# Constant scales for all f16 halves with one verdict at the end, a new order for batch 0, and batch 2's attention weights as f16 halves

## The chip, the cores and the metric

One NeuronCore of a Trainium2 chip runs the whole program. The metric is the time of one execution on the device in microseconds, the median of several runs. In the profile PE is TensorE (matmul), PEld its weight loads, DVE VectorE, ACT ScalarE, POOL GpSimd and SP SyncE, whose queue issues nearly all DMAs.

## The reference

```python
# q, k, v: (8, 12, 448, 64) f32; w_in: (768, 2048), w_out: (2048, 768) f64
scores = scale * np.matmul(q, k.transpose(0, 1, 3, 2)) - np.log(S)
attn = 1.0 / (1.0 + np.exp(-scores))
x = np.matmul(attn, v)             # then (8 * 448, 768)
h = x @ w_in
g = h - np.tanh(h)
out = g @ w_out
```

Attention with a sigmoid in place of a softmax feeds a two-layer product. h is small here, so h - tanh(h) needs far more than f16's precision, and the weights come as f64.

## The kernel before

A factor of a product is held either as f32, or as two f16 halves, high = f16(s·t) and low = f16(s·t - high), with a scale s. A product of two factors in halves takes three f16 matmuls (high·high, high·low, low·high), a product of f32 factors one f32 matmul, which the trace shows as two instructions. Making halves takes two elementwise operations: the high part (`split`, `parts`, `prep_v`, `halves`, mostly on ACT, some on DVE) and the low part (a SCALAR_TENSOR_TENSOR on DVE).

The scale of every such tensor is computed from its data. For w_in and w_out, `conv_end` sums absolute values or columns with a matmul for each converted piece (`cs`, L303, 24 pieces; `wl`, L297, 32 pieces), and `w_in_scales`, `w_out_scale` and `scale_of` make a power of two from it. For q, k and v, `norm` takes sums of squares on ACT, and `scales` makes the scales of two head pairs with a matmul (`pbn`, L478) and a chain of small DVE operations. For x, `token_norms` (`nm`, L826) and `x_scale` do it, for g `g_scales`. The scales are tiles of [128, 1], which the operations read as operands.

The program runs batch after batch. In batch 0 (`first`) the weights come in and are turned from f64 to f32 (`convert`: `conv_load`, `conv_sign` on ACT, `conv_bits` on DVE), while batch 0's attention runs in f32 (`attention32`). Then `mixture` makes g from eight blocks of w_in: the first FP32 = 6 blocks with f32 matmuls (L1264), the other two with f16 halves (`product`, L953), for which x and w_in are split before. `moe2` is the second product (`po`, L1156). From batch 1 on, `moe2` of batch b is interleaved with the attention of batch b+1 (`stream`, cut into steps called blocks), and the first product is done by `moe1` (batch 1) or `moe1_quarters` (from batch 2 on, `py`, `px`, L1003), which reads w_in's combinations from DRAM into a ring (`load_ring`, L158). `combine` makes these combinations during batch 1.

AV32 = 3 says that in batches 0, 1 and 2 the attention weights times v are f32 matmuls (the `a`, `vn` form of L559). From batch 3 on the weights are split (`split_a`, L545 and L546) and v too (`prep_v`), and three f16 matmuls take the place of one.

Each engine runs its instructions in program order. What sets that order: for batch 0 the string ORDER, one letter a step (s scores, v weights times v, r a piece of w_in, R a piece of w_out, M half a block of the mixture, t a step of g's curve, q halves of x, S and Z halves of w_in, A and a halves of w_out, P a part of moe2, B a step of the next batch's attention, C a late piece of w_out, n, w, y, g, x, b, X steps of the scales); for the others the tables BLOCKS, BLOCKS1, TAIL, MADE, FILL and PARTS, which give the place of a step among moe2's matmuls in microseconds. Scores and the mixture's blocks share two PSUM buffers (`sc`): a block's buffer comes free when both ACT (`u`, L1119) and DVE (`m`, L1121) have read it.

At the end `verdict` compares the largest h with a limit, and a flag decides whether `General`, a slow f32 version of everything, runs after it.

Of the kernel before, what the change touches and what calls it, by code (L numbers as in the profile page):

```python
# [20 lines left out]
D = 64  # L21
QT = 3
A_SCALE = 2.0**15
TINY = 2.0**-120
CUT = 0.65


# [9 lines left out]
class Builder:  # L37

    AV32 = 3

    EARLY = 4
    LAND = ("o", "o", 2, "v", "v", "v", 1, 0, 3, 4, 5, "o", "o", 2, "v", "v", "v", 1, 0, "o")
    ORDER = (
        "lurmlorumsrrsrrmmlussmvvrrssvvrlrssvvrrvruvlssrurssvvrrssvlrrsvvvursrsvs"
        "vrrssvrsrrvvvvRrRrRRRMrRRRnRrRRGMRRwtMttRtRBtwRRtMwBgttMtRtRttDMBttRtRtt"
        "DMtyqqMBBtRttqRqMtBttqqMttSSDMtRxStRtBRAStMtttSADMtBttSMttAttAttMMtAPPta"
        "RRBPtBbtCaBCBACPtFCCPBPCPPBPPCBCPPBCBCPPCCBPCCCPBCCCPCXBaaAPaPPPBAPaaaBB"
        "PPSPSZPSZSPPPPPPSPBPPZPPPNPZPSPZSSNNPPSZPZSSPPPP"
# [3 lines left out]
    TAIL = (1, 2, 4.5, 5)  # L52
    MADE = (6, 9, 12.5, 15, 18, 22, 25, 29, 31, 34)
# [5 lines left out]
    BLOCKS1 = (4, 7, 8, 11, 13, 16, 20, 20, 20, 27, 32, 36, 36, 36, 43, 47, 51, 52)  # L59

    TP = 8
    FP32 = 6
# [3 lines left out]
    AWAY = (1, 3)  # L66

# [3 lines left out]
    def __init__(self, ctx, tc, q, k, v, w_in, w_out, out):  # L71
# [20 lines left out]
        self.ident = self.const.tile([P, P], F32, name="ident")  # L92
        make_identity(nc, self.ident)
        self.identb = self.const.tile([P, P], BF16, name="identb")
        nc.vector.tensor_copy(self.identb, self.ident)
        self.onesf = self.const.tile([P, P], F32, name="onesf")
        nc.vector.memset(self.onesf, 1.0)
# [80 lines left out]
    def combine(self):  # L178
# [74 lines left out]
    def conv_sign(self, p):  # L253
# [7 lines left out]
        else:  # L261
            pool, tag, bufs = self.xp, "x", 8
            if p["when"] == "mixture" and p["k"] % 3:
                pool, tag, bufs = (self.xp, "x2", 2) if p["k"] % 3 == 1 else (self.nat, "vn", 2)
# [21 lines left out]
    def conv_end(self, p):  # L286


        nc = self.nc
        kind, r, i, n = p["piece"]  # L290
        high = p["a"].bitcast(BF16).rearrange("p (n t) -> p n t", t=2)[:, :, 1]
        if kind == "out":
            start = r == (self.EARLY if p["when"] == "product" else 0)
            stop = r == (self.EARLY - 1 if i and p["when"] == "mixture" else self.NF - 1)
            if start:
                self.wl = self.ps.tile([P, 512], F32, name="wl", tag="mm", bufs=2)
            nc.tensor.matmul(self.wl[:, :n], self.onesb, high, start=start, stop=stop)  # L297
            if stop:
                self.sums_out[i].append(self.wl)
            return  # L300
        if r == 0:
            self.cs = self.ps.tile([P, 512], F32, name="cs", tag=("av", "tr")[i % 2], bufs=1)
        nc.tensor.matmul(self.cs[:, :n], self.identb, high, start=(r == 0), stop=(r == self.NC - 1))  # L303
        if r == self.NC - 1:
            sq = self.sm.tile([P, n], BF16, name="sq", tag="sq", bufs=4)
            nc.scalar.activation(sq, self.cs[:, :n], AF.Square)
            self.row.append(sq)

    def convert(self, pieces, when):

        ps = [{"piece": q, "k": k, "when": when} for k, q in enumerate(pieces)]
        wait, end = [None, None], [None, self.conv_end]
        if when == "mixture":
            wait, end = [None] * 3, [None] + end
        elif when == "product":
            wait, end = [None], [None, None] + end
        stages = [self.conv_load] + wait + [self.conv_sign, self.conv_bits] + end
# [23 lines left out]
    def split_w_in(self):  # L341

        for n in range(0, self.NC * self.NB, 2):
            self.split_rows(self.wi, n, self.Swi)
            yield 1

    def scale_of(self, total, tag, unit=2.0**49):

        nc = self.nc
        t = self.sm.tile([P, 1], F32, name=tag + "_t")  # L350
        nc.vector.tensor_scalar(t, total, 2.1, TINY, op0=ALU.mult, op1=ALU.max)
        y = self.pow2(t, 1, tag)
# [1217 lines left out]
```

## Time and profile before

| | |
|---|---|
| median of 3 runs | 1125.9 us (1125.8 to 1128.17) |
| the profiled execution | 1125.58 us, span 1123.7 us |
| PE busy | 1113.8 us (99%) |
| DVE, ACT, POOL busy | 780.3, 781.9, 70.8 us |
| from the start to the first mixture matmul | 50.7 us |
| mixture, then moe2 of batch 0, to 215.4 us | 164.7 us |
| moe1 of batch 1, to 269.9 us | 54.5 us |
| moe2 of batch 1 with batch 2's attention, to 361.8 us | 91.9 us |

The span goes from the first instruction to the last. Busy time of PE is modelled, since matmuls overlap in the array; the time from one matmul's start to the next says more. A row of the timeline that stands for several instructions gives their first start and their total.

### The profile page before, as it was taken

Reading aid. Unit: us, or ns where it says so; the run is one execution under the profiler, and the core shown is the slowest. Engines: PE = TensorE matmul, PEld = TensorE weight load, DVE = VectorE, ACT = ScalarE, POOL = GpSimd, SP = SyncE. Lnnn points to the kernel's source line nnn. Section 1 sums busy time; section 2 is a strip of 40 time slices with the busy share of each in tenths; the row PEclk is TensorE's granted clock in tenths of the full one; section 3 lists DMA queues with packets and bytes.
Section 4 is the critical chain, followed back from the end, with each engine's and each line's share of the span. In section 5 each row is a group of like instructions: output and inputs, shape, how many; then the busy total and the mean of one; then the engine's idle time right before and its main releaser. Section 6 shows DMA issues by size and latency. Waiting matters only on the chain.

```text
span 1123.7 us, 20080 instructions
## 1 busy us (share of the span) xinstructions
PE 1113.8 (99%) x8067; PEld 671.8 (60%) x8072; DVE 780.3 (69%) x1376; ACT 781.9 (70%) x1269; POOL 70.8 (6%) x54
## 2 busy tenths in 40 slices
PE   9999999999999999999999999999999999999997
PEld 3355444554445984469644894449844696449953
DVE  6989888697466666787578865887768775655710
ACT  7967895466777569886788767886698867655600
POOL 0000000000000002200021000200022000200000
PEclk9999999999999999999999999999999999999999
DMA  9992262284544742236324543247512670036200
GB/s 367 393 361 63 88 196 71 87 230 131 188 161 161 250 164 69 75 111 241 115 67 131 182 148 129 72 162 242 185 59 75 201 256 21 17 99 230 99 25 28
DMA packets 78694, 167.13 MB, mean 149 GB/s; under 512 B 24320, under 2 KB 58240, under 8 KB 71808
## 3 DMA queue, kind: packets, MB, share of 16 engines
q1 hardware_dynamic: 78304, 165.42, 43.7%
q8 instruction: 65, 1.06, 0.4%
q10 hardware_dynamic: 288, 0.34, 0.1%
q14 instruction: 37, 0.30, 0.1%
HBM read 137.43 MB, written 28.31 MB: 147 GB/s over the span
## 4 chain that ended last, share of the span: by engine, by line
PE 89%; DVE 7%; ACT 2%; issue 1%; DMA 1%; DVEq 0%; SPq 0%; ACTq 0%
PE po L1156 35%; PE py L1003 12%; PE px L1003 10%; PE acc L559 9%; PE sc L528 9%; PE ph L953 6%; PE ph L1264 5%; DVE wi L334 3%; DVE ahl L546 2%; DMA wi<-w 1%; ACT sqn L469 1%; PE cs L303 1%; PE warm L115 1%; ACT a L539 1%; PE wl L297 1%
## 5 line engine op out<-in xcount | busy, mean ns | idle before, releaser
L1156 PE MATMUL po<-g,wo 128*128 128x448 f16 x2304 | 451.9, 353 | 0.0
L1156 PEld LDWEIGHTS <-wo 128*128 128x128 f16 x2304 | 219.3, 98 | 221.7 <-issue 26.7
L1003 PEld LDWEIGHTS <-wi 128*128 128x128 f16 x3024 | 289.8, 98 | 6.6 <-issue 1.5
L546 DVE SCALAR_TENSOR_TENSOR ahl<-a,ahl 128x896 f16<-128x896 f32 x105 | 135.0, 1320 | 95.4 <-ACT ahl L545 94.3
L539 ACT ACTIVATE a<-sc,nls,rn 128x896 f32<-128x896 f32 x147 | 155.7, 1089 | 59.0 <-PE sc L528 58.9
L1003 PE MATMUL py<-wi 128*128 128x224 f16 x1728 | 181.8, 259 | 1.9 <-DMA wi<-w 1.0
L1003 PE MATMUL px<-wi 128*128 128x224 f16 x1296 | 140.4, 259 | 0.0
L947 DVE SCALAR_TENSOR_TENSOR g<-m,Sg,g 128x896 f16<-128x896 f32 x64 | 73.6, 1150 | 44.7 <-ACT g L946 44.6
L528 PE MATMUL sc<-Q,K 64*128 64x448 f16 x1008 | 100.6, 353 | 0.0
L545 ACT ACTIVATE ahl<-a 128x896 f16<-128x896 f32 x105 | 94.3, 941 | 0.5
L1013 ACT ACTIVATE u<-py,ih 128x448 f32<-128x448 f32 x48 | 30.4, 634 | 77.7 <-DVE py L1084 77.7
L946 ACT ACTIVATE g<-m,Sg 128x896 f16<-128x896 f32 x64 | 66.2, 1034 | 13.6 <-DVE m L1027 11.1
L528 PEld LDWEIGHTS <-K 64*128 64x128 f16 x1008 | 35.5, 97 | 58.6 <-issue 34.5
L559 PE MATMUL acc<-ahl,vhl 128*64 128x448 f16 (+1 forms) x720 | 67.2, 356 | 0.0
L590 POOL TENSOR_TENSOR x<-x 128x448 f32<-128x448 f32 x20 | 22.8, 1139 | 599.1 <-ACT x L573 599.1
L1264 PE MATMUL ph<-x,wi 128*128 128x448 f32 x144 | 55.8, 540 | 0.0
L1016 DVE SCALAR_TENSOR_TENSOR m<-px,ihk,u 128x448 f32<-128x448 f32 x48 | 32.8, 683 | 32.6 <-ACT u L1013 32.6
L953 PEld LDWEIGHTS <-wi 128*128 128x128 f16 x360 | 35.2, 98 | 33.2 <-issue 0.5
L953 PE MATMUL ph<-xhl,wi 128*128 128x448 f16 x288 | 54.6, 352 | 0.0
L559 PE MATMUL acc<-a,vn 128*64 128x448 f32 (+1 forms) x288 | 54.4, 553 | 0.0
L599 POOL TENSOR_TENSOR x<-x,x 128x448 f32<-128x448 f32 x21 | 35.3, 1682 | 298.3 <-ACT x L588 297.1
L1027 DVE SCALAR_TENSOR_TENSOR m<-q,m 128x896 f32<-128x896 f32 x48 | 52.0, 1084 | 0.7
(186 smaller groups left out, 1218.3 us busy)
## 6 DMA issues: line engine op xcount, KB each, us to landing
wi<-w SPq DMA_DIRECT2D x53, 1344.0 KB, 6.1
out<-o SPq DMA_DIRECT2D x47, 224.0 KB, 2.0
knn<-k SPq DMA_DIRECT2D x45, 224.0 KB, 2.6
qnn<-q SPq DMA_DIRECT2D x44, 224.0 KB, 3.1
rawo<-moe_w_out SPq DMA_DIRECT2D x23, 384.0 KB, 4.7
raw<-moe_w_in SPq DMA_DIRECT2D x13, 512.0 KB, 8.2
vn<-v SPq DMA_DIRECT2D x24, 256.0 KB, 2.9
w<-wi SPq DMA_DIRECT2D x16, 384.0 KB, 5.9
```

The lines of the kernel that those rows point to most:

```text
L528: self.nc.tensor.matmul(ps[i * m : (i + 1) * m, h, : self.S], K[i][r, w, c * P : c * P + m], Q[i][r, x, :], start=(n == 0), stop=(n == len ...
L539: self.nc.scalar.activation(a[:, 0], ps[:, :, : self.S], AF.Sigmoid, bias=self.nls, scale=scale)
L545: nc.scalar.activation(A[:, 0], a[:, 0], AF.Copy, scale=A_SCALE)
L546: nc.vector.scalar_tensor_tensor(A[:, 1], a[:, 0], A_SCALE, A[:, 0], op0=ALU.mult, op1=ALU.subtract)
L559: self.nc.tensor.matmul(acc[i][h * D : (h + 1) * D, : self.S], v[k, w, 2 * QT + h if half else h * QT + c], A[k, x, h], start=(n == 0 and ...
L946: nc.scalar.activation(g[:, 0], m, AF.Copy, scale=Sg)
L947: nc.vector.scalar_tensor_tensor(g[:, 1], m, Sg, g[:, 0], op0=ALU.mult, op1=ALU.subtract)
L953: self.nc.tensor.matmul(ph, self.wi[:, self.slot(c, k), part, e * P : (e + 1) * P], xhl[c][:, x, :], start=(i == 0), stop=(i == len(prods) ...
L1003: nc.tensor.matmul(out, w[:, a, c, i], x[:, b, c, j], start=start and k == 0, stop=k == len(prods) - 1, skip_group_check=True,)
L1027: V.scalar_tensor_tensor(d["m"], d.pop("q"), C0, d["m"], op0=ALU.add, op1=ALU.mult)
L1156: nc.tensor.matmul(po[:, :S], self.wo[:, e * self.NF + rows[f // 2][f % 2], w, at : at + P], moving(gs[f // 2][:, x], f % 2), start=(f == ...
L1264: nc.tensor.matmul(ph[:, e, :S], self.fp32(self.wi, self.slot(c, k))[:, 0, e * P : (e + 1) * P], xs[c], start=(c == 0), stop=(c == self.NC ...
```

## The change

All scales become constants of the class: KQ = 2^6 for q and k, VS = 2^8 for v, XS = 2^12 for x, WS = 2^10 for w_in, OS = 2^11 for w_out and GS = 2^22 for g. With them go `conv_end`, `pow2`, `scale_of`, `w_in_scales`, `w_out_bound`, `w_out_scale`, `scales`, `x_scale`, `h_scales` and `g_scales`. The sums of squares of q, k and v stay, but go to a tile `seen` that only `verdict` reads; those of v are now taken in batch 1 too, and those of w_out by eight squares in the last batch (`check_w_out`). `verdict` has eight conditions instead of one.

The operations that read a scale from a tile now have it as a number in the instruction. The high halves of q and k move: ten of 84 stay on ACT (QA, KA), the others are on DVE (before: all 42 of q and 4 of k on ACT). The squares of x that POOL multiplied and added are now made on ACT and added on DVE in pairs (`squares`). AV32 becomes 2 and FP32 becomes 4, with ORDER and BLOCKS1 rewritten.

```diff
-    AV32 = 3
+    AV32 = 2
+    QA = (1, 2, 4, 6, 8)
+    KA = (0, 1, 4, 5, 11)
...
-    FP32 = 6
+    FP32 = 4
...
+    KQ = 2.0**6
+    VS = 2.0**8
+    XS = 2.0**12
+    GS = 2.0**22
+    WS = 2.0**10
+    OS = 2.0**11
...
-    def conv_end(self, p):
...
-            nc.tensor.matmul(self.wl[:, :n], self.onesb, high, start=start, stop=stop)
...
-        nc.tensor.matmul(self.cs[:, :n], self.identb, high, start=(r == 0), stop=(r == self.NC - 1))
...
-    def scales(self, ss, where):
...
-    def add_squares(self, j, x, pool):
+    def squares(self, j, x, b):
...
+            if j % 2 == 0:
+                self.x2 = self.xp.tile([P, 2, self.S], BF16, name="x2", tag="x2", bufs=3)
+            x2 = self.x2[:, j % 2]
+        self.nc.scalar.activation(x2, x, AF.Square)
...
+        elif j % 2:
+            self.nc.vector.tensor_tensor(self.x2s, self.x2s, self.x2, op=ALU.add)
...
-                K[g] = self.parts(qk[g][0], sc[g][0][:, 0:1], "K", g < NP and g not in (2, 3))
+                K[g] = self.parts(qk[g][0], self.KQ, "K", g in self.KA)
...
-                Q[g] = self.parts(qk[g][1], sc[g][0][:, 1:2], "Q", True)
+                Q[g] = self.parts(qk[g][1], self.KQ, "Q", g in self.QA)
...
-            aa = [self.weigh(pss[0], sc[g][1][:, 0:1])]
+            aa = [self.weigh(pss[0], weight)]
...
+    def check_w_out(self):
...
+            self.nc.scalar.activation(
+                t, self.wo[:, i * n : (i + 1) * n, 0], AF.Square, accum_out=self.seen_out[:, i : i + 1]
+            )
...
-            events.append((20, self.verdict))
+            checks = self.check_w_out()
+            events += [(6 + 4 * n, lambda: next(checks)) for n in range(self.NF // 2)]
+            events.append((42, self.verdict))
```

PE in a stretch of batch 0's attention (sc scores, acc weights times v, cs the matmul of `conv_end`), before:

```order
L559 MATMUL acc<-a_242,vn 64x448 x2
L559 MATMUL acc<-a_247,vn 64x448 x2
L303 LDWEIGHTS identb
L303 MATMUL cs<-sta,identb 128x512
L303 LDWEIGHTS identb
L303 MATMUL cs<-sta,identb 128x512
L559 MATMUL acc<-a_282,vn 64x448 x2
```

and now:

```order
L480 MATMUL acc<-a_224,vn 64x448 x2
L480 MATMUL acc<-a_229,vn 64x448 x2
L480 MATMUL acc<-a_262,vn 64x448 x2
L480 MATMUL acc<-a_267,vn 64x448 x2
L449 MATMUL sc<-qnn,knn 128x448 x4
L449 MATMUL sc<-qnn,knn 64x448 x2
```

The cs matmuls that stood between the matmuls of attention are gone.

DVE in the mixture (m and g are the curve's steps and its low half, stb and wo the conversion of w_out, wi the low half of w_in, un to rn the scales of q and k), before:

```order
L933 TENSOR_SCALAR g_765<-g_765 128x1
L122 TENSOR_SCALAR g_y<-g_765 128x1
L936 TENSOR_SCALAR iSg<-g_y 128x1
L938 RECIPROCAL Sg<-iSg 128x1
L1121 SCALAR_TENSOR_TENSOR m<-ph,ihk_117,u 128x896
L947 SCALAR_TENSOR_TENSOR g<-m,Sg,g 128x896
L1127 SCALAR_TENSOR_TENSOR m<-q,m 128x896
```

and now:

```order
L986 SCALAR_TENSOR_TENSOR m<-ph,u 128x896
L815 SCALAR_TENSOR_TENSOR g<-m,g 128x896
L992 SCALAR_TENSOR_TENSOR m<-q,m 128x896
L305 SCALAR_TENSOR_TENSOR wi<-wi 128x2x256
L268 SCALAR_TENSOR_TENSOR stb<-stb,rawo 128x384
L276 SCALAR_TENSOR_TENSOR wo<-rawo,stb 128x384
L305 SCALAR_TENSOR_TENSOR wi<-wi 128x2x256 x2
```

The one-column operations are gone, and more halves of w_in stand between the curve's steps: from the first m<-ph to the eighth there are 98 instructions before and 72 now; 13 instead of 6 of them are halves of w_in.

ACT in batch 2's attention (a the sigmoid, ahl the high half of a weight tile, sqn the sums of squares), before:

```order
L571 ACTIVATE x_2954<-acc 128x448
L588 ACTIVATE x_2956<-x_2954 128x448
L539 ACTIVATE a_2978<-sc,nls,rn 128x896
L503 ACTIVATE Q<-qnn,sn 128x448
L469 ACTIVATE sqn,ss_121<-knn 128x448
```

and now:

```order
L494 ACTIVATE x_2820<-acc 128x448
L508 ACTIVATE x_2822<-x_2820 128x448
L466 ACTIVATE ahl<-a_2781 128x896
L466 ACTIVATE ahl<-a_2786 128x896
L1038 ACTIVATE o<-po 128x448
L460 ACTIVATE a_2867<-sc,nls 128x896
L424 ACTIVATE K<-knn 128x448
L466 ACTIVATE ahl<-a_2867 128x896
L417 ACTIVATE sqn,seen<-knn 128x448
```

A high half follows each sigmoid: from the last curve of moe1 to the last output of batch 1 there are 25 ahl on ACT instead of 6, and one high half of q instead of seven.

## Rows read from the trace of the kernel before

**Rows 1.** The page, busy time of each engine.
```profile
PE 1113.8 (99%) x8067; PEld 671.8 (60%) x8072; DVE 780.3 (69%) x1376; ACT 781.9 (70%) x1269; POOL 70.8 (6%) x54
```

**Rows 2.** The chain that ended last, in order of time: start us, us, what.
```profile
92.28 13.53 PE ph L1264 x36
...
215.42 54.48 PE ph L953 x288
...
315.32 2.41 PE acc L559 x12
...
329.07 3.32 PE acc L559 x20
...
424.64 1.82 PE acc L559 x18
...
438.37 2.52 PE acc L559 x30
```

**Rows 3.** Busy us by stage: PE, PEld, DVE, ACT, POOL; granted clock, DMA share, GB/s.
```profile
10.50:50.70 40.20, 40.20 (x202) 12.07 (x199) 36.10 (x63) 36.84 (x54) 0.00 (x0) 1.00 1.03 400
63.50:124.50 61.00, 61.00 (x210) 30.93 (x209) 53.69 (x100) 45.57 (x77) 0.00 (x0) 1.00 0.48 152
124.50:215.40 90.90, 90.85 (x560) 39.58 (x559) 70.83 (x135) 66.30 (x110) 5.24 (x4) 1.00 0.37 112
269.90:361.80 91.90, 91.90 (x595) 40.04 (x594) 51.84 (x102) 67.51 (x111) 4.76 (x4) 1.00 0.45 152
413.40:494.20 80.80, 80.80 (x574) 38.33 (x572) 59.49 (x104) 68.60 (x112) 12.11 (x8) 1.00 0.24 75
```

**Rows 4.** PE's timeline in batch 0: start us, us, instructions.
```profile
21.12 0.62 PE L303 MATMUL cs<-sta,identb 128*128 128x512 bf16 x2
21.67 0.97 PE L559 MATMUL acc<-a,vn 128*64 128x448 f32 x4
...
50.74 4.67 PE L1264 MATMUL ph<-x,wi 128*128 128x448 f32 x12
```

**Rows 5.** Groups by form, PE's scale matmuls: count, busy us, mean ns, idle us.
```profile
L297 PE MATMUL wl<-stb,onesb 128*128 128x384 bf16 x32 | 8.2, 332 | 0.1
L303 PE MATMUL cs<-sta,identb 128*128 128x512 bf16 x23 | 7.6, 393 | 0.0
L478 PE MATMUL pbn<-ss,onesb 128*128 128x6 bf16 x15 | 2.5, 168 | 0.0
```

**Rows 6.** DVE's timeline: the first of 15 scale operations, and what follows them.
```profile
73.04 0.16 DVE L378 TENSOR_SCALAR W<-pb 128x1 f32<-128x1 f32 x1 [1.67 <-PE pb L376]
...
75.52 1.13 DVE L1121 SCALAR_TENSOR_TENSOR m<-ph,ihk,u 128x896 f32<-128x896 f32 x1
```

**Rows 7.** Groups by form: sigmoids, high halves of weights, low halves of w_in.
```profile
L539 ACT ACTIVATE a<-sc,nls,rn 128x896 f32<-128x896 f32 x147 | 155.7, 1089 | 59.0 <-PE sc L528 58.9
L545 ACT ACTIVATE ahl<-a 128x896 f16<-128x896 f32 x105 | 94.3, 941 | 0.5
L539 ACT ACTIVATE a<-sc,nls 128x896 f32<-128x896 f32 x21 | 20.3, 1001 | 4.8 <-PE sc L528 4.8
L334 DVE SCALAR_TENSOR_TENSOR wi<-wi,swi_s 128x512 f16<-128x512 f32 x24 | 17.2, 748 | 4.3 <-ACT wi L331 4.1
```

**Rows 8.** DVE's timeline, low halves of weights without and with POOL at work.
```profile
352.86 2.09 DVE L546 SCALAR_TENSOR_TENSOR ahl<-a,ahl 128x896 f16<-128x896 f32 x2 [1.56 <-ACT ahl L545]
...
442.42 3.55 DVE L546 SCALAR_TENSOR_TENSOR ahl<-a,ahl 128x896 f16<-128x896 f32 x2
```

**Rows 9.** PE's timeline at the start of batch 2: a wait for the ring.
```profile
374.58 1.90 PE L1003 MATMUL py<-wi 128*128 128x224 f16 x18 [0.97 <-DMA wi<-w]
```

**Rows 10.** POOL's timeline beside the second row of rows 8.
```profile
443.16 1.86 POOL L599 TENSOR_TENSOR x<-x,x 128x448 f32<-128x448 f32 x1
```

**Rows 11.** The stretches after the last matmul, columns as in rows 3.
```profile
1118.00:1120.00 2.00, 0.00 (x0) 0.00 (x0) 0.05 (x1) 0.00 (x0) 0.00 (x0) 1.00 0.44 129
...
1122.00:1123.70 1.70, 0.00 (x0) 0.00 (x0) 0.00 (x0) 0.00 (x0) 0.00 (x0) 0.50 0.05 14
```

More of the change, by code (lines that the diff above doesn't have):

```diff
@@ L23 @@
 A_SCALE = 2.0**15
-TINY = 2.0**-120
 CUT = 0.65
@@ L284, in conv_bits @@
         )
-    def conv_end(self, p):
[L289 to L296, printed above, removed]
-            nc.tensor.matmul(self.wl[:, :n], self.onesb, high, start=start, stop=stop)
[L298 to L302, printed above, removed]
-        nc.tensor.matmul(self.cs[:, :n], self.identb, high, start=(r == 0), stop=(r == self.NC - 1))
[L304 to L307, printed above, removed]
     def convert(self, pieces, when):
         ps = [{"piece": q, "k": k, "when": when} for k, q in enumerate(pieces)]
-        wait, end = [None, None], [None, self.conv_end]
+        wait = [None, None]
         if when == "mixture":
-            wait, end = [None] * 3, [None] + end
+            wait = [None] * 3
         elif when == "product":
-            wait, end = [None], [None, None] + end
-        stages = [self.conv_load] + wait + [self.conv_sign, self.conv_bits] + end
+            wait = [None]
+        stages = [self.conv_load] + wait + [self.conv_sign, self.conv_bits]
         for t in range(len(ps) + len(stages) - 1):
@@ new lines, in verdict @@
+        low = self.sm.tile([P, 1], F32, name="low")
+        high = self.sm.tile([P, 3], BF16, name="lowb")
+        wo = self.sm.tile([P, 2], F32, name="wosum")
+        V.tensor_scalar(self.seen, self.seen, self.QKV_MOST, None, op0=ALU.is_le)
+        V.tensor_reduce(low, self.seen, axis=AX.X, op=ALU.min)
+        V.tensor_copy(high[:, 0:1], low)
+        V.tensor_reduce(wo[:, 0:1], self.seen_out, axis=AX.X, op=ALU.add)
+        V.tensor_scalar(wo[:, 1:2], wo[:, 0:1], self.O_RANGE[1], None, op0=ALU.is_le)
@@ new lines, in verdict @@
+        V.tensor_copy(high[:, 1:3], wo)
+        total = self.ps.tile([P, 512], F32, name="total", tag="av", bufs=1)
+        self.nc.tensor.matmul(total[:, :3], self.onesb, high, start=True, stop=True)
+        V.tensor_scalar(ok[:, 0:1], total[:, :1], P - 0.5, None, op0=ALU.is_ge)
+        V.tensor_scalar(ok[:, 1:2], self.xmin, self.X_RANGE[0], None, op0=ALU.is_ge)
+        V.tensor_scalar(ok[:, 2:3], self.xmax, self.X_RANGE[1], None, op0=ALU.is_le)
+        V.tensor_scalar(self.xmin, self.xmin, self.W2x, 1.06, op0=ALU.mult, op1=ALU.mult)
@@ new lines, in verdict, with split_w_out @@
+        V.tensor_reduce(self.xmax, ok, axis=AX.X, op=ALU.min)
+    def check_w_out(self):
+        n = 4
+        for i in range(2 * self.NF // n):
+            t = self.tp.tile([P, n, self.HALF], BF16, name="wosq", tag="t", bufs=self.TP)
+            self.nc.scalar.activation(
+                t, self.wo[:, i * n : (i + 1) * n, 0], AF.Square, accum_out=self.seen_out[:, i : i + 1]
+            )
+            yield 1
+    def split_w_out(self):
+        for n in range(0, 2 * self.NF, 2):
+            self.split_rows(self.wo, n, self.OS)
@@ L772, in stream @@
             norms(g + 4)
+            while raw:
+                t, i = raw.pop(0)
+                self.norm(t, self.seen[:, 3 * i + 2 : 3 * i + 3])
             yield 2750, True
@@ L1245, in first @@
         self.rest = self.split_w_in()
-        bound = self.w_in_scales()
+        self.ahead = self.split_w_out()
         products = self.moe2(0, self.gs)
```

301 lines of the change are left out of this document (73 added, 228 removed).

## The prediction

> **What bounds the kernel now.** I read the busy times first: PE 99%, DVE 69%, ACT 70% [rows 1]. Busy time of PE is modelled, so the next view is the chain of waits, to see how fast PE really goes. In it 288 f16 matmuls of 448 columns take 54.48 us, 189 ns each; 36 f32 instructions take 13.53 us, 376 ns each [rows 2]. 448 columns at the higher of TensorE's two levels, 2.4 GHz, are 187 ns. So a busy PE is here a PE at its rate, and the end of the program is set by the sum of its matmuls.
>
> The page Perfetto Trace Analysis of the Trainium skill (Identifying the Most-Contended Engine) says that matmul busy time is no measure of the distance from the limit, and that the weight loads' share is a better one. By it the 60% of PEld would leave PE room, and taking work off PE need give nothing; the 189 ns in the chain decide against that here.
>
> The third view is busy time by stage [rows 3]. It tells where another engine is close behind PE. In batch 0's attention (10.5 to 50.7 us) PE is busy 40.2 us of 40.2, ACT 36.8, DVE 36.1, and the DMA share is 1.03. In the mixture (63.5 to 124.5) DVE is busy 53.7 us of 61.0. In batch 2's attention (269.9 to 361.8) ACT is busy 67.5 of 91.9 and DVE 51.8. In the same stage of a later batch (413.4 to 494.2) ACT is busy 68.6 of 80.8 with no idle time on PE, so 85% on ACT is harmless there.
>
> **What comes off PE.** The 24 cs matmuls: two take 0.55 us from the first's start to the next instruction [rows 4], 0.28 us each, 6.7 us; the group's busy time of 7.6 us for 23 [rows 5] is the upper bound. The 32 wl matmuls: 384 columns at the pace of the chain's 448 in 189 ns would be 0.16 each, the group's busy time is 8.2 us for 32, 0.26 each [rows 5]; I take 0.19, 6.1 us. The 21 pbn matmuls: 2.5 us for 15 as busy time, 3.5 for all [rows 5]; they overlap their neighbours, I take 0.07 each, 1.5 us. The few other scale matmuls, six of them small: 0.7 us. Two block pairs of the mixture become f16: a pair is 24 f32 instructions of 376 ns, 9.0 us, and becomes 36 of 189 ns, 6.8 us [rows 2]; two give 4.4 us. Batch 2's weights times v: two head pairs take 2.41 + 3.32 us as f32 (32 instructions) and 1.82 + 2.52 us as f16 halves (48) [rows 2]; 1.39 us less, three times a batch, 4.2 us. The verdict adds one matmul of three columns. Its DVE operations wait for nothing later than the squares of w_out that ACT makes 8 us of moe2 earlier, so I cost it at nothing; if PE had to wait for them it would be some ten operations of 0.17 us [rows 6], under 2 us. The sum is 23.6 us: against the profiled execution's 1125.58 us a floor of **1102.0**.
>
> **What the other engines give back.** Four places.
>
> Batch 0's attention. PE loses 22 cs between 10.5 and 50.7 us, 6.2 us, and has 34.0 us of work left there. ACT loses only three short squares and keeps about 35 us; DVE keeps its conversion of w_in, 36.1 us, but its early pieces are all that the first mixture blocks need. So ACT comes first now, and the matmuls of attention wait for sigmoids. I give back 2.5 us (bounds: 1.0, which is ACT's 35 without a gap, and 6.2, nothing gained). DMA is at its full rate in this stretch too; its loads stay the same and attention's stand early in the queue, so I cost it at nothing beside ACT.
>
> The mixture. PE's part falls by about 7 us to 54 (4.4 for the blocks, 2 to 3 for wl). On DVE 32 one-column scale operations and two reductions go: 15 of them take 2.48 us [rows 6], 0.17 each, so 5.3 us and about 1 more. Seven low halves of w_in come in, 0.75 us each [rows 7], 5.2 us, and one high half of q. DVE therefore keeps about 53 us, less what a scale as a number saves. That saving has a row on ACT: the same sigmoid takes 1089 ns with a scale tile and 1001 without [rows 7]. For some 30 operations on DVE I estimate between 0 and 2 us. So DVE becomes as long as PE here, and starts later: its conversion of w_in fills 36.1 of the 40.2 us before the mixture and still runs into it, while PE starts the mixture some 4 us earlier. The two shared PSUM buffers let PE run about one block ahead of DVE's m, 7 to 9 us, which covers most of it. I give back 2.0 us (0 to 6).
>
> Moe2 of batch 0 with batch 1's attention. ACT has 66.3 us of 90.9 [rows 3], crowded in the first 40. It loses three high halves of q and gains six pairs of v's squares. I give back 1.0 us (0 to 3).
>
> Batch 2's attention. PE's part falls from 91.9 to about 87. ACT gains 19 high halves of 0.9 us [rows 7] and loses six high halves of q and 0.09 us on each of 21 sigmoids: 67.5 + 17 - 4 - 2 makes 78 to 80 us, 90% or more, where the later batches run at 85%. DVE gains 19 low halves of 1.05 us [rows 8], the halves of v and of q, and loses its chains: 51.8 to about 73 us, 84%. I give back 1.5 us (0 to 6, the price of holding ACT at 85%).
>
> What is won besides: PE waited 0.97 us for the ring at the start of batch 2 [rows 9], and a batch's first product no longer waits for x's scale. 1.0 us at most for both, of which the ring's part can also grow; I take 0.7. In batches 3 to 7 PE keeps its work but for the pbn. ACT gains four squares of x a batch and loses six high halves of q, DVE the reverse of about the same size, and POOL falls silent: two low halves that take 2.09 us take 3.55 while POOL multiplies and adds [rows 8, 10], so DVE gains some microseconds that PE does not wait for. I cost these batches at nothing beyond pbn; the cover is ACT's 12 idle us and DVE's 21 in 80.8.
>
> Together 1102.0 + 2.5 + 2.0 + 1.0 + 1.5 - 0.7 = 1108.3 us, that is **1108**. The profiled execution lies 0.3 us under the median, so the same number stands for the median.
>
> **Rivals.**
>
> *PE stays saturated, 1102 (1100 to 1104).* For it: in the whole trace PE is idle 9.9 us (1123.7 less 1113.8), 5.7 of them in the tail after 1118.0 [rows 1, 11]. Against: it was kept full by matmuls that waited for nothing in attention, and those are what goes. 0.15.
>
> *ACT and DVE become the bound in batch 0 and batch 2's attention, 1117 (1112 to 1121).* The order still has them at 90% or more. It gives back all of the 6.2 us of the first stage, 6 in the mixture (DVE keeps the 7.3 idle us that it had there: 53 + 7 = 60 instead of 54), and 3 in batch 2's: 1102 + 15. Against: DVE's idle time in the mixture was mostly waiting for PE. 0.22.
>
> *TensorE's clock falls in batch 0's attention: slower.* Place: the first 50 us, where PE would be idle 10 to 15% of the time in many short gaps. The granted clock is 1.00 in every stage, is still 1.00 from 1118 to 1120, when PE is idle, and 0.50 in the last 1.7 us [rows 3, 11], the lower level of 1.2 GHz. At that level each us of PE work costs one more. The 34 us of that stage would make 1108 + 34 = 1142; from 20 us of work at the lower level on, the gain is gone. The page TensorE: Matmul & The Clock Gate (What's actually happening) says that the throttled state is the default and activity releases it; the rows at the end agree. Against: I expect no gap longer than 2 us there, and a ring wait of 0.97 us with the clock at 1.00 is in the trace. 0.03.
>
> *The verdict fails, and General runs after everything.* From the reference's inputs the largest h squared is 0.023 to 0.026, between the limits 0.012 and 0.04, and the other sums lie well inside theirs. Its 192 f32 matmuls a batch of 0.75 us alone would add over 1100 us. 0.01.
>
> *No change that can be told,* since something unseen takes over: 0.02.
>
> **How the numbers follow.** The forecast, 1104 to 1112, has 0.57. The range must reach into both neighbours: 1102 is PE's sum with nothing given back, 1117 the middle of the second rival. Faster by over 0.2% (2.3 us, about what a measurement of this kernel can tell from no change) are the forecast and the first two rivals, 0.94; same 0.02; slower, the clock and the verdict, 0.04.
>
> **What would show it.** Right: PE's busy time near 1090 us, the first mixture matmul at 46 to 48 us instead of 50.7 [rows 4], the first of batch 1's moe1 about 11 to 14 us earlier than 215.4, the end of moe2 of batch 1 some 17 us earlier than 361.8, later batches of 131 us as before; idle time on PE before acc and sc in the first 50 us named as ACT's, and before ph as DVE's m. Wrong: the mixture no shorter than before, ACT named in front of acc for more than 5 us between moe1 and batch 2, a granted clock under 1.00 in the first 50 us, or a gain spread over batches 3 to 7.

## The result, and the profile after

The changed kernel takes 1106.92 us (median of 4, 1105.72 to 1107.35) against 1125.97 for the one before, a ratio of 0.9825 (95% interval 0.9808 to 0.9842). The forecast was 1108, the range 1101 to 1117. The profiled execution takes 1105.72 us against 1125.58, so the two traces differ by what is to be explained, 19.9 us.

The starts of PE's matmuls, read from its timeline in both traces, cut that into stretches. They go from the start of one matmul to the start of another, so they can differ by 0.2 us from the table of the kernel before. The last column has the prediction's terms, sorted into the same stretches.

| stretch | before | after | difference | predicted |
|---|---|---|---|---|
| start to the first mixture matmul | 50.74 | 48.38 | -2.4 | -6.2 + 2.5 = -3.7 |
| mixture and moe2 of batch 0 | 164.5 | 152.8 | -11.7 | -12.0 + 3.0 = -9.0 |
| moe1 of batch 1 | 54.5 | 54.5 | 0 | 0 |
| moe2 of batch 1 with batch 2's attention | 92.1 | 90.1 | -1.9 | -4.4 + 1.5 = -2.9 |
| first product of batch 2 | 49.0 | 47.4 | -1.6 | -0.7 |
| from there to the last matmul | 705.9 | 703.6 | -2.2 | -1.0 |
| sum | | | -19.9 | -17.3 |

The forecast lies 1.1 us above the median. Between the two traces it predicted 17.3 us and 19.9 came. The stretches were off in both directions: two together gained 2.3 us less than predicted, three together 4.8 us more. So the closeness of the sum is in part luck.

Busy times on the page of the changed kernel, which answer to [rows 1]: PE has lost 22.8 us and is still at 99%.

```profile
PE 1091.0 (99%) x8061; PEld 664.8 (60%) x8061; DVE 734.5 (67%) x1205; ACT 757.6 (69%) x1289; POOL 0.2 (0%) x4
```

Busy time by stage, columns as in [rows 3], for batch 0's attention, the mixture, batch 2's attention and the same stage of a later batch:

```profile
10.50:48.40 37.90, 34.00 (x175) 10.08 (x173) 33.00 (x58) 34.62 (x50) 0.00 (x0) 1.00 1.03 402
62.00:114.10 52.10, 52.10 (x215) 26.58 (x214) 50.52 (x75) 44.51 (x80) 0.00 (x0) 1.00 0.76 231
255.60:345.80 90.20, 88.96 (x640) 41.40 (x639) 70.61 (x111) 77.56 (x126) 0.00 (x0) 1.00 0.45 149
395.80:476.60 80.80, 80.80 (x572) 38.13 (x570) 53.96 (x91) 64.45 (x108) 0.00 (x0) 1.00 0.25 75
```

The work is what the prediction said (PE 34.0 us in the first row, ACT 77.6 in the third), but PE is busy all of the mixture beside a DVE at 97%. All that PE waits for in the whole trace, from the view of its waits (us in total, times, the longest):

```profile
PE sc L449 <- ACT a L460: 3.8, 2, 2.4
PE warm L119 <- DVE nls L1065: 1.0, 1, 1.0
PE acc L480 <- DVE ahl L467: 1.0, 2, 0.6
```

The second row is the start of the program, the third lies in batch 2's attention, the first in batch 0's. PE's timeline there:

```profile
24.35 0.59 PE L449 MATMUL sc<-qnn,knn 64*64 64x448 f32 x2 [1.45 <-ACT a L460]
...
28.11 1.92 PE L449 MATMUL sc<-Qn,Kn 64*128 64x448 f32 x8
32.40 1.02 PE L449 MATMUL sc<-qnn,knn 64*128 64x448 f32 x4 [2.37 <-ACT a L460]
33.36 0.98 PE L480 MATMUL acc<-a,vn 64*64 64x448 f32 x8
34.27 1.02 PE L449 MATMUL sc<-qnn,knn 64*128 64x448 f32 x4
35.22 2.48 PE L480 MATMUL acc<-a,vn 128*64 128x448 f32 x12
...
48.38 4.78 PE L1121 MATMUL ph<-x,wi 128*128 128x448 f32 x12
```

And ACT's timeline before the second wait:

```profile
26.47 0.70 ACT L260 ACTIVATE sta<-raw 128x512 f32<-128x512 f32 x1 [0.45 <-DMA raw<-moe_w_in]
27.07 1.89 ACT L460 ACTIVATE a<-sc,nls 128x896 f32<-128x896 f32 x2
28.85 0.68 ACT L260 ACTIVATE sta<-wo 128x512 f32<-128x512 f32 x1
30.78 0.67 ACT L260 ACTIVATE sta<-raw 128x512 f32<-128x512 f32 x1 [1.25 <-DVE sta L270]
31.35 1.00 ACT L460 ACTIVATE a<-sc,nls 128x896 f32<-128x896 f32 x1
```

The scores were ready at about 30 us. The sigmoid that frees their buffer starts at 31.35, because two steps of the conversion stand ahead of it in ACT's queue, and the second waits 1.25 us for a buffer that DVE still reads. So ACT's 34.6 us are not the bound of this stretch; their order is.

The chain that ended last has most of the mixture in two long pieces without a gap between them: 84 of its 96 f32 instructions and then 108 of its 144 f16 matmuls, 376 and 189 ns each as in [rows 2]:

```profile
54.29 31.57 PE ph L1121 x84
85.86 20.43 PE ph L821 x108
```

The groups that answer to [rows 7] and [rows 8]: the sigmoid without a scale tile, and the low half of the weights with POOL silent.

```profile
L460 ACT ACTIVATE a<-sc,nls 128x896 f32<-128x896 f32 x168 | 161.1, 999 | 64.5 <-PE sc L449 63.3
L467 DVE SCALAR_TENSOR_TENSOR ahl<-a,ahl 128x896 f16<-128x896 f32 x126 | 132.6, 1088 | 98.6 <-ACT ahl L466 98.5
```

### The profile page after: what moved, and what is told of

It reads as the page before. It is cut to its first block, busy times and chain, and to the rows that moved or that the text cites. A ratio compares the mean times of both kernels' runs of the same rounds, so it can differ in the third digit from the quotient of the medians.

```text
span 1103.9 us, 19772 instructions
## 1 busy us (share of the span) xinstructions
PE 1091.0 (99%) x8061; PEld 664.8 (60%) x8061; DVE 734.5 (67%) x1205; ACT 757.6 (69%) x1289; POOL 0.2 (0%) x4
## 4 chain that ended last, share of the span: by engine, by line
PE 96%; DVE 2%; ACT 1%; issue 1%; ACTq 0%
PE po L1018 39%; PE py L869 15%; PE px L869 11%; PE acc L480 10%; PE sc L449 9%; PE ph L821 7%; PE ph L1121 3%; PE warm L119 1%; DVE sta L271 0%; DVE ahl L467 0%; PE nm L735 0%; DVE sta L270 0%; ACT ahl L466 0%; ACT sqn L417 0%; ACT a L460 0%
## 5 line engine op out<-in xcount | busy, mean ns | idle before, releaser
L460 ACT ACTIVATE a<-sc,nls 128x896 f32<-128x896 f32 x168 | 161.1, 999 | 64.5 <-PE sc L449 63.3
L466 ACT ACTIVATE ahl<-a 128x896 f16<-128x896 f32 x126 | 113.0, 938 | 0.5
L815 DVE SCALAR_TENSOR_TENSOR g<-m,g 128x896 f16<-128x896 f32 x64 | 69.7, 1090 | 41.1 <-ACT g L814 41.1
L879 ACT ACTIVATE u<-py 128x448 f32<-128x448 f32 x48 | 26.1, 544 | 77.9 <-DVE py L950 77.9
L814 ACT ACTIVATE g<-m 128x896 f16<-128x896 f32 x64 | 60.4, 944 | 11.2 <-DVE m L893 10.6
L480 PEld LDWEIGHTS <-vhl 128*64 128x64 f16 (+1 forms) x864 | 38.7, 108 | 42.0 <-issue 21.7
L893 DVE SCALAR_TENSOR_TENSOR m<-q,m 128x896 f32<-128x896 f32 x48 | 52.0, 1083 | 0.6
L882 DVE SCALAR_TENSOR_TENSOR m<-px,u 128x448 f32<-128x448 f32 x48 | 29.9, 624 | 32.5 <-ACT u L879 31.9
L890 ACT ACTIVATE q<-u,b 128x896 f32<-128x896 f32 x48 | 49.6, 1034 | 0.4
L1038 ACT ACTIVATE o<-po 128x448 f32<-128x448 f32 x27 | 14.4, 533 | 38.6 <-PE po L1018 26.8
L949 DVE TENSOR_TENSOR px<-px,pu 128x224 f32<-128x224 f32 x48 | 19.2, 399 | 30.8 <-PE px L869 30.8
```

The lines of the kernel that those rows point to most:

```text
L460: self.nc.scalar.activation(a[:, 0], ps[:, :, : self.S], AF.Sigmoid, bias=self.nls, scale=scale)
L466: nc.scalar.activation(A[:, 0], a[:, 0], AF.Copy, scale=A_SCALE)
L480: self.nc.tensor.matmul(acc[i][h * D : (h + 1) * D, : self.S], v[k, w, 2 * QT + h if half else h * QT + c], A[k, x, h], start=(n == 0 and ...
L814: nc.scalar.activation(g[:, 0], m, AF.Copy, scale=Sg)
L815: nc.vector.scalar_tensor_tensor(g[:, 1], m, Sg, g[:, 0], op0=ALU.mult, op1=ALU.subtract)
L890: nc.scalar.activation(d["q"], d.pop("u"), AF.Square, bias=self.b0)
```

## The experiments

**What the scales cost the later batches (e1, e2).** After batch 2's first product, every batch from 3 to 5 is 0.56 us shorter, 0.53 of it in the first product and 0.03 in the attention stage (80.83 to 80.80); batch 6 is 0.53 shorter. The prediction had put this on the pbn matmuls. Two kernels take one chain of scales each out of the kernel before, and leave the scale tiles as operands.

```diff
 def x_scale(self, m):          # e1
-    ...
+    return self.Sxc, self.ixc
 def scales(self, ss, where):   # e2
-    ...
+    return self.sc_, self.rc_
```

> The kernel before with x's scale as a constant (the four small DVE operations of x_scale are gone, the operands stay tiles). In the trace of before PE loses 0.13 + 0.31 + 0.22 + 0.13 us at four places of every first product from batch 2 on, 0.8 us a batch; in the trace after, none of them. Theory 1, the chain of x's scale made the operations at a batch's start late: about 0.4 to 0.8 us a batch in six batches come off, 1121 to 1123.5 us against 1126. Rival, the chains of the scales of q, k and v, and the dearer operations with a scale tile, made them late: within 1 us of before. The prediction's own term for this (with the ring's wait 0.7 us in all) is with the rival.

> The kernel before with constant tiles for the scales of q, k and v: the 21 pbn matmuls, their relu on ACT and their DVE chains of six small operations are gone, the sums of squares and the scale tiles as operands stay. Prediction's term: pbn is 1.5 us of PE, so 1124.4. Theory 1 (from the starts of the matmuls around it, pbn costs PE 0.03 to 0.1 us, and x's scale made the first products late): 0.2 to 0.8 us less, 1125 to 1126. Rival, the q, k and v chains made the first products late: 2.5 to 4.5 us less, 1121.5 to 1123.5, and the four short waits of every first product are gone.

Measured: e1 1125.84, ratio 0.9996 (0.9986 to 1.0005), no change; e2 1122.98, ratio 0.9970 (0.9957 to 0.9982), 3.6 us less than the 1126.57 of before. PE's timeline at the start of batch 3's first product, in e1:

```profile
494.19 3.75 PE L995 MATMUL py<-wi 128*128 128x224 f16 x36
...
498.64 2.19 PE L995 MATMUL py<-wi 128*128 128x224 f16 x18
```

and in e2:

```profile
492.60 3.62 PE L981 MATMUL py<-wi 128*128 128x224 f16 x36
...
496.92 1.89 PE L981 MATMUL py<-wi 128*128 128x224 f16 x18
```

In e1 the two groups are as long as before (3.74 and 2.20 us); in e2 they have lost 0.12 and 0.31. Theory 1 fell, the rival holds for these two places. The second group waits for x's last low halves (wi), which DVE makes. DVE's timeline of before has the chain of q's, k's and v's scales, six small operations, ahead of them:

```profile
489.09 0.15 DVE L484 TENSOR_TENSOR un<-tn 128x3 f32<-128x3 f32 x1
...
489.83 0.15 DVE L495 TENSOR_SCALAR rn<-n_y 128x1 f32<-128x1 f32 x1
...
498.57 1.87 DVE L334 SCALAR_TENSOR_TENSOR wi<-x,Sx,wi 128x448 f16<-128x448 f32 x3
```

and that of e2 has not:

```profile
496.11 1.87 DVE L334 SCALAR_TENSOR_TENSOR wi<-x,Sx,wi 128x448 f16<-128x448 f32 x3
```

The halves start 4.4 us behind the first product's start before and 3.5 in e2; DVE has no gap between the chain and them. The 0.12 us of the first group stand in front of a matmul that the trace of before has waiting for ACT's copy of moe2's output (o). That copy starts 1.19 us behind the product's start before and 1.07 in e2, where the chain's own operation on ACT (tn) no longer stands ahead of it. x's own chain has the same kind of operations but stands earlier, where DVE has slack. And the pbn matmuls were next to nothing: e2's attention stage takes 80.80 us, as in the changed kernel. The other two of the four places that the expectation counted are as long in e2 as before. The one of 0.22 us is no wait but a matmul of `norm_sums`, and it is in the changed kernel too; the last one lost 0.09 us in the changed kernel alone, and no run shows why.

In batch 2 the ring's wait [rows 9] is gone in e2 too (49.0 us for the first product, up to the first matmul of moe2, became 47.4). But that wait varies between executions: it is 0.2 to 0.9 us in other kernels here, and 0.5 in e11, which is the changed kernel once more, whose first product of batch 2 takes 0.65 us longer for it. So the part of the ring in these 1.6 us, about 1 us, is not shown to come from the change.

**What batch 2's f16 halves are worth (e3).**

```diff
-    AV32 = 2
+    AV32 = 3
```

> The changed kernel with AV32 = 3 again: batch 2's weights times v as f32 matmuls, without its halves of the weights and of v and without v's squares. Theory 1 (PE's sum decides, and 2.1 us of the 4.2 us that the halves save are given back as waits for the low halves): 2.1 us slower than the changed kernel's 1106.9, so 1109, with no wait on PE between 255 and 346 us. The prediction's terms (4.2 saved, 1.5 given back): 2.7 us slower. Rival, ACT and DVE were the bound of that stage with the halves: no difference from 1106.9, or faster.

Measured: 1109.77 (ratio 0.9848, 0.9830 to 0.9867), 2.9 us over the changed kernel. Batch 2's stage, columns as in [rows 3], has PE busy throughout:

```profile
257.40:349.50 92.10, 92.10 (x591) 39.80 (x590) 48.06 (x84) 62.98 (x111) 0.00 (x0) 1.00 0.45 151
```

92.1 us against 90.1: the halves are worth 2.0 us there, of the 4.2 that they save on PE. That is theory 1. The profiled execution is 4.2 us longer than that of the changed kernel; most of what is left, 1.7 us, came from batch 0. Batch 0 of this kernel is that of the changed kernel, instruction by instruction, and yet its mixture starts at 50.09 us instead of 48.38. When PE goes on after its second wait for a sigmoid, it is only 0.13 us behind. PE's timeline from there, and windows of 2 us:

```profile
32.53 1.49 PE L449 MATMUL sc<-qnn,knn 64*128 64x448 f32 x4 [2.24 <-ACT a L460]
33.96 1.77 PE L480 MATMUL acc<-a,vn 64*64 64x448 f32 x8
35.66 1.35 PE L449 MATMUL sc<-qnn,knn 64*128 64x448 f32 x4
```

```profile
32.00:34.00 2.00, 1.47 (x8) 0.35 (x8) 1.90 (x5) 1.38 (x2) 0.00 (x0) 0.74 1.02 393
34.00:36.00 2.00, 2.00 (x12) 0.60 (x12) 0.69 (x1) 1.25 (x2) 0.00 (x0) 0.50 1.04 400
36.00:38.00 2.00, 2.00 (x10) 0.64 (x10) 0.46 (x2) 1.97 (x5) 0.00 (x0) 0.91 0.97 351
```

Behind a wait of 2.24 us the granted clock falls to 0.50, the lower level of 1.2 GHz, and is back within some 4 us. From one group's start to the next's, four sc matmuls take 1.43 us instead of the 0.96 of the changed kernel, eight acc 1.70 instead of 0.91, and four sc 1.28 instead of 0.95: 1.6 us.

**What makes PE wait in batch 0's attention (e4).** Five letters r of ORDER, each a step of the conversion, moved behind sigmoids:

```diff
-...rrvruvlssrurssvvrrsssvlrrsv...
+...rrvuvlssrurssrvvsssrrvlrrsv...
```

> The changed kernel with two pieces of batch 0's conversion moved behind the sigmoids that PE waits for (5 letters r of ORDER between places 40 and 60 moved by two to four places). Theory 1 (a sigmoid stands behind conversion steps in ACT's queue, which wait for DMA or DVE, and so PE's score buffers come free late, 1.45 and 2.37 us): PE's idle time before sc falls from 3.8 to 1.5 us or less and the time by 1.5 to 2.5 us, 1104.4 to 1105.4. Rival, ACT's work of 34.6 us in the stage's 37.9 is the bound: the waits move to later sigmoids and the gain is under 0.7 us. Second rival, the conversion of w_in on DVE comes late: the first mixture blocks wait for wi, and the time is the same or longer.

Measured: 1104.38 (1104.06 to 1104.79), ratio 0.9806 (0.9790 to 0.9822), 2.5 us less than the changed kernel (1.8 of it before the mixture; this execution was 0.7 us behind at 11.5 us, ahead of the moved letters). PE's waits in e4:

```profile
PE acc L480 <- DVE ahl L467: 1.0, 2, 0.6
PE sc L449 <- ACT a L460: 0.8, 2, 0.4
```

The wait for sigmoids went from 3.8 to 0.8 us, the mixture starts at 46.56. Theory 1 holds; the same ACT work (34.3 us) fits into 36.1 us. The conversion was not late for the mixture.

**How close DVE is in the mixture (e6).** From here on e4 is the base. The low half of g is made twice in batch 0, 8.7 us more on DVE.

```diff
+        for _ in range(1 if self.xready else 2):
             nc.vector.scalar_tensor_tensor(g[:, 1], m, Sg, g[:, 0], ...)
```

> The kernel of e4 with the low half of g made twice in all eight blocks of batch 0's mixture: eight more DVE operations of 1.09 us, 8.7 us. Theory 1 (DVE runs at 50.5 of 52.1 us in the mixture, right behind PE, but nothing waits for it as long as it stays behind): the margin is 1.5 to 3 us, the other 5 to 7 us come out as waits of PE before ph or later, 1109.5 to 1111.5 against 1104.4. Rival, the low halves of w_in and of w_out that fill DVE there can all be done later: under 2 us slower. The second rival of the prediction (DVE is already the bound) would make it the whole 8.7 us, 1113.

Measured: 1111.16, ratio 0.9876 (0.9852 to 0.9900), 6.8 us over e4; batch 1's moe1 starts 6.75 us later. Among PE's waits there is a new one:

```profile
PE ph L822 <- DVE wi L305: 3.7, 3, 2.7
```

In the median 2.0 of the 8.7 us are hidden, as theory 1 expected. But not all of the 6.8 is time that PE waited for DVE. Behind the longest wait the clock falls here too:

```profile
111.19 7.15 PE L822 MATMUL ph<-wo,wi 128*128 128x448 f16 x28 [2.75 <-DVE wi L305]
```

```profile
110.00:115.00 5.00, 3.81 (x12) 1.61 (x13) 4.97 (x8) 3.32 (x5) 0.00 (x0) 0.66 0.14 56
```

These 28 matmuls take 7.0 us to the next group's start, where 28 of 189 ns are 5.3: 1.7 us. On the other side the slowest of the four executions (1113.18) is 8.8 us over e4, so that it hides nothing. What is shown is that DVE is no bound of the mixture in e4, and that it is at most a few us away from being one.

**The cs matmuls back (e8).** The 24 of them in e4, one step behind the conversion.

```diff
+            nc.tensor.matmul(self.cs_[:, :n], self.onesb, self.last, start=..., stop=...)
```

> The kernel of e4 with the 24 cs matmuls of w_in's conversion back (128x512 bf16, as before one step behind the conversion; nothing reads their sums). Prediction's term: 0.28 us each, 6.7 us of PE, of which in the changed kernel only 2.4 us became time, because PE waited 3.8 us for sigmoids. Theory 1 (in e4 PE waits about 1.2 us less than 2.5 there): 4.5 to 5.7 us slower than 1104.4, 1109 to 1110, and PE's idle time before sc is gone. Rival, they stand where PE would wait anyway: under 3 us slower.

Measured: 1121.97, ratio 0.9966 (0.9951 to 0.9981), 17.6 us over e4. Both theories failed. PE now waits for DVE's conversion, in front of the cs matmuls:

```profile
PE cs L280 <- DVE sta L271: 8.1, 7, 2.1
```

and the clock falls in three places, here around 43 us:

```profile
42.00:44.00 2.00, 1.24 (x5) 0.30 (x4) 1.91 (x4) 0.46 (x1) 0.00 (x0) 0.89 0.75 260
44.00:46.00 2.00, 2.00 (x6) 0.53 (x6) 1.93 (x4) 1.01 (x1) 0.00 (x0) 0.50 0.79 248
```

The mixture starts 18.9 us later: 6.7 for the matmuls, 8.1 for the waits for DVE, and a rest of 4.1 that goes with the lower clock and is not taken apart. In the order of before the same matmuls stood where their data was ready. What they cost in an order that is not written for them says little about what they cost before; e4 answers that better.

**POOL (e7).** x's squares of batches 1 to 7 on POOL instead of ACT.

```diff
-        self.nc.scalar.activation(x2, x, AF.Square)
+        self.nc.gpsimd.tensor_tensor(x2, x, x, op=ALU.mult)
```

> The kernel of e4 with x's squares of batches 1 to 7 on POOL instead of ACT (42 multiplications; ACT has 0.58 us less each). Theory 1 (POOL slows DVE while it works, and PE waits for DVE nowhere in the later batches): two low halves of the weights take 3 us or more instead of 2.1 where POOL runs beside them, the later batches keep 131.1 us, the time is within 1.5 us of 1104.4, the rest from batch 2's attention, where PE waits for the low halves already. Rival, POOL's silence is a part of the gain of the later batches (0.56 us a batch): 2 to 4 us slower.

Measured: 1103.94, ratio 0.9808 (0.9786 to 0.9829), the same as e4; a later batch takes 131.1 us. This gives POOL back 42 of the 70.8 us that it worked before; with that much, the rival is out: POOL's silence is no part of the gain. But the low halves of the weights hardly meet POOL here; the halves of x's combinations do. POOL's and DVE's groups in e7:

```profile
L511 POOL TENSOR_TENSOR x<-x 128x448 bf16<-128x448 f32 x42 | 42.1, 1002 | 939.4 <-ACT x L494 763.4 <-ACT x L492 176.0
...
L467 DVE SCALAR_TENSOR_TENSOR ahl<-a,ahl 128x896 f16<-128x896 f32 x126 | 133.6, 1095 | 86.4 <-ACT ahl L466 86.2
...
L305 DVE SCALAR_TENSOR_TENSOR wi<-xt,wi 128x672 f16<-128x672 f32 x12 | 13.4, 1160 | 0.0
```

the last group in e4:

```profile
L305 DVE SCALAR_TENSOR_TENSOR wi<-xt,wi 128x672 f16<-128x672 f32 x12 | 9.7, 853 | 0.0
```

and one of the places in e7's timelines:

```profile
472.13 2.36 DVE L305 SCALAR_TENSOR_TENSOR wi<-xt,wi 128x672 f16<-128x672 f32 x2
472.81 0.96 POOL L511 TENSOR_TENSOR x<-x 128x448 bf16<-128x448 f32 x1 [13.86 <-ACT x L494]
```

The mean of 1160 ns hides two values: seven of the twelve take 0.85 us, as in e4, and five take 1.59. Each of the five starts while a POOL operation runs; here it starts at 472.90 and POOL has 0.87 us to go, and it takes 0.74 us longer than without. The Trainium skill (SBUF — State Buffer, section "SBUF: two separate sides") says that DVE, in an operation with two inputs from SBUF, and POOL take a shared port in turn, each for a whole instruction. These five operations agree; no run here tells the port from another cause.

**Batch 2's attention (e5, e9, e12).** PE loses 2.1 us there, in three groups: from start to start 30 acc take 3.73 us instead of 2.52, 18 take 2.43 instead of 1.82, and 12 sc 1.56 instead of 1.24. Of this 1.0 us is named as waits for low halves, and the rest is a slower pace of the same matmuls. e5 moves two steps out of the way:

```diff
-    MADE = (6, 9, 12.5, 15, ...)
+    MADE = (6, 11.5, 12.5, 15, ...)
...
-            norms(g + 3)
             keep(g, (2, QT), aa)
+            norms(g + 3)
```

> The kernel of e4 with two steps moved that stand in front of batch 2's halves of the weights: the squares of q and k (which only the verdict reads, 1.1 us on ACT) behind them, and one step of the combinations of w_in (four operations, 2.3 us on DVE) from place 9 to 11.5 among moe2's matmuls. Theory 1 (PE's waits of 0.6 and 1.2 us for the low halves between 255 and 346 us, and 0.3 at a score, come from what stands ahead of the halves in the queues): the stretch from the end of moe1 of batch 1 to the first product of batch 2 falls from 90.1 us to 88.3 to 89.0, the time from 1104.4 to 1102.6 to 1103.3. Rival, ACT's sum (77.6 of 90.2 us) is the bound there: the waits move, under 0.5 us gained. A move in the later batches of more than 0.3 us each is expected by neither.

Measured: 1105.52, ratio 0.9822 (0.9802 to 0.9843), 1.1 us slower than e4; the stretch takes 92.1 us. Neither theory expected a loss. On ACT a copy now waits for the step that was moved on DVE, and PE for the sigmoids behind it:

```profile
276.19 0.84 ACT L191 ACTIVATE wt<-wi 128x768 f16<-128x768 f32 x1 [2.27 <-DVE wi L203]
```

The clock falls to 0.50 behind PE's wait of 2.45 us here too (12 sc and 30 acc behind it take 1.6 us more than the 1.24 and 2.52 above). e9 moves the next two steps of the combinations as well:

```diff
-    MADE = (6, 11.5, 12.5, 15, ...)
+    MADE = (6, 11.5, 14, 16.3, ...)
```

> The kernel of e5 with the two steps of the combinations behind the moved one placed later as well (14 and 16.3 in place of 12.5 and 15 among moe2's matmuls). In e5 ACT stood 2.27 us in front of a copy of the combination that DVE now made later, and PE waited 2.45 us for the sigmoids behind it. Theory 1 (what stands ahead in the in-order queues makes PE wait, not ACT's sum): ACT's wait of 2.27 us is gone, the stretch from moe1 of batch 1 to the first product of batch 2 takes 88.5 to 89.5 us (90.1 in e4, 92.1 in e5), the time 1102.9 to 1103.9. Rival, ACT's sum is the bound there: 90 us or more, 1104.4 or slower.

Measured: 1108.42, ratio 0.9836 (0.9823 to 0.9849); the stretch takes 95.7 us. The time lies where the rival put it, but the cause is another than ACT's sum. ACT's wait is gone; the last of the moved steps also issues the load of the next combination, and DVE stands in front of it with everything behind:

```profile
293.08 0.56 DVE L202 TENSOR_TENSOR wi<-wi 128x384 f32<-128x384 f32 x1 [5.14 <-DMA wi<-w]
```

The load is issued at 288.34 us instead of 283.35 in e4. So these steps stay. e12 is e4 with the squares alone behind the halves:

```diff
-            norms(g + 3)
             keep(g, (2, QT), aa)
+            norms(g + 3)
```

> The kernel of e4 with the squares of q and k alone behind the halves of the weights; the combinations of w_in stay where they were. In e9 DVE stood 5.14 us in front of a combination whose load came later by the later steps, so those steps can't move; the squares have no such load behind them. Theory 1: the second wait of PE for a low half (1.2 us between 255 and 346 us) falls by 0.6 to 1.1 us, the first (0.6) stays; the stretch from moe1 of batch 1 to batch 2's first product takes 89.0 to 89.6 us against 90.1, the time is 1103.3 to 1104.0. Rival, the wait has another cause: 90.1 us and 1104.4.

Measured: 1102.26 (1101.86 to 1103.91), ratio 0.9791 (0.9777 to 0.9804). The stretch takes 89.1 us, PE's waits are:

```profile
PE sc L449 <- ACT a L460: 0.8, 2, 0.4
PE acc L480 <- DVE ahl L467: 0.4, 1, 0.4
```

The 30 acc take 2.61 us again. Theory 1 holds: 1.1 us of squares that nothing waits for, ahead of halves that PE waits for, cost PE 1.0 us. ACT's sum was not the bound, it is 77.6 us in both. The other 1.1 us that PE loses in this stretch are still there. The median is 1.0 us below the expected range and 2.1 below e4. Between the two profiled executions 1.0 us of this lies in the stretch; the rest lies before the mixture (0.3), in the first product of batch 5 (0.4) and behind the last matmul (0.4), and nothing ties that to the edit. e12 is the fastest kernel of this study, 4.7 us below the changed one in the medians and 3.9 between the profiled executions.

**Does the clock fall in the changed kernel too (e10, e11)?** e10 fills the longest wait with six matmuls on constants; e11 is the changed kernel again.

```diff
-...vvrrsssvl...
+...vvrrssfsvl...
+            "f": lambda: self.warm(6, "av", 1),
```

> The changed kernel with six idle matmuls (128x512 bf16 on constants, 1.3 us, nothing reads them) put on PE in front of the score in batch 0 for which it waits 2.37 us; no step is moved. In the executions of e3, e5, e6 and e8 the granted clock fell to 0.50 for 2 to 4 us behind such a wait of 2.2 us or more, in the profiled execution of the changed kernel it did not. Theory 1 (the clock falls behind that wait in most executions of the changed kernel too, which costs 1.1 us as in e3): with the wait cut to about 1.1 us the clock stays at 1.00, and the median falls by 0.6 to 1.2 us below the changed kernel's of the same call. Rival, the wait alone counts: the median is the same within 0.3 us, or later by the filler.

> The changed kernel once more, beside the two others of this call. Theory 1 of e10: its executions lie in two groups 1.1 us apart (with and without the fall of the clock behind the wait of 2.37 us), median 1106 to 1107.5. Rival: one group, as the kernels without a long wait have (e4: 0.7 us from the lowest to the highest of four).

Measured: e10 1106.27 (1105.22 to 1106.30), ratio 0.9817 (0.9804 to 0.9831); e11 1106.21 (1105.44 to 1107.19), ratio 0.9820 (0.9807 to 0.9834). The medians are the same, as the rival said: the fill costs as much as it may save (e10's mixture starts 0.3 us later than e11's). By the rows of e3 a fall would cost 1.6 us there, not the 1.1 that theory 1 took. The profiled execution of e11 has the wait of 2.2 us and a clock of 1.00 behind it. Of its five, the two slowest (1106.80 and 1107.19) have a mean granted clock of 0.997, the others 0.998 or 0.999; that fits a fall in some executions, but only the profiled one has a trace, so how often it falls stays open.

## Why the prediction was right, and where its terms were not

**PE's sum: right.** PE's busy time fell to 1091.0 us where "near 1090" was expected. Added up from start to start in the trace of before, the wl matmuls took 6.2 us (6.1 taken), cs in the attention stage 6.2 (6.2), the other scales of w_in 0.75 (0.7). No run puts these back one by one; that they became time is read from the two traces, in which PE has no gap in the mixture. The two pairs of the mixture gave 9.0 - 6.8 us each, as taken.

**pbn: wrong term.** "I take 0.07 each, 1.5 us": the attention stage lost 0.03 us a batch, and e2 without them 0.03. The gain came at a place that the prediction left at nearly nothing, "a batch's first product no longer waits for x's scale. 1.0 us at most": it is 0.53 us in each of batches 3 to 5. Of that e2 shows 0.43, and with it that the gain hangs on the q, k and v chains, not on x's (e1). In batch 2 it is 1.6 us with the ring, whose part comes and goes between executions. Together 2.2 us were forecast for the two, 3.8 came. A gain spread over batches 3 to 7 was one of the prediction's signs of being wrong; 2.2 us came that way, from a wait that it had put at nearly nothing.

**Batch 0's attention: mechanism right, price too low.** "I give back 2.5 us" (1.0 to 6.2) was 3.8. The mixture started at 48.38, outside the 46 to 48 that the prediction named. Its reason, ACT comes first, is only half of it: e4 shows that ACT's sum leaves room, and that two steps stood wrongly in its queue.

**The mixture and moe2 of batch 0: wrong.** "I give back 2.0 us" and "1.0" were both nothing. What went from PE in this stretch, added up from start to start, is 11.7 us, and the stretch is 11.75 us shorter. The prediction was right that DVE becomes about as long as PE (97% of the mixture, and e6 leaves it a few us at most), but a busy share near PE's is not yet a wait: PE waited for DVE nowhere in it. PE also came only 2.4 us earlier than before, not 4.

**Batch 2's attention: near in size, not in its reason.** 1.5 us were forecast, 2.1 given back (e3: 2.0 us left of 4.2). For 1.0 us of it the cause is again the order, not the 78 us of ACT that the prediction argued from (e12). For the other 1.1 the cause stays open: e5 and e9, which were to find it, made new waits.

**The rivals.** *PE saturated, 1102*, has the number of e12 (1102.26), but by chance: e12 still gives back 3 us in the two attention stages, and about as much came from the first products of batches 2 to 6, which that sum left out. *ACT and DVE the bound* did not come true; in the mixture e6 shows that a few us more on DVE would have done it. *The clock* was argued away with "I expect no gap longer than 2 us there"; there was one of 2.37. In the profiled execution of the changed kernel the clock stayed at 1.00; in e3 it fell behind the same wait and cost 1.6 us, not 34, because it was back some 4 us after PE went on. *The verdict* did not fail, and `General` did not run: the verdict's matmul takes its place among moe2's at 1083 us, and from the last matmul's start to the end it is 7.1 us, as before with 7.0.

## What to carry to other kernels

- When a saturated engine loses work, first look at what stands in the queues ahead of the instructions that it will wait for. Here sums of busy time (85 to 95% on ACT and DVE) said little about the waits; two small reorderings gave 2.5 and 2.1 us in the medians with the same work, 1.8 and 1.0 of it traced to the waits that they were made for.
- A chain of small operations costs by its place: six on DVE ahead of an operand that PE needs next cost 0.3 us a batch, x's four where DVE has slack cost nothing. Before a step is moved, ask which load it issues and who waits for that.

## What the hardware did that was not expected

- The granted clock fell to 0.50 behind single waits of PE of 2.2 to 2.8 us (e3, e5, e6) and behind shorter ones in e8 (2.1 us, 1.8 us, and two of 1.4 us with 0.4 us of work between them). It was at 1.00 again some 4 us after PE went on, and one such fall cost 1.6 to 1.7 us (e3, e5, e6). Behind waits of 2.2 and 2.37 us in the changed kernel (e11 and the result) it stayed at 1.00. In e9 it was still at 1.00 behind a wait of 2.2 us and fell only 6 us later, behind further waits of 0.4 and 1.6. So in these runs the length of one wait does not tell whether the clock falls. The Trainium skill (TensorE: Matmul & The Clock Gate, section "HAM oscillation — how this bites in real kernels") says that waits between stretches of matmuls bring the lower clock back; the rows of e3 agree, and those of the changed kernel show that such a wait need not.
- A scale as a number in the instruction instead of a tile saved some 60 ns on DVE, whatever the width: the low half of g went from 1150 to 1090 ns, and an operation half as wide from 683 to 624. On ACT it saved 90 ns of a sigmoid's 1089, as [rows 7] had shown.
